# Two decode layers: w2's last block read over 96 partitions, and one load of V per layer split into 112 rows and four groups of 4 rows

## The chip, the core and the metric

One Trainium2 chip, one of its cores. The metric is the device time of one execution in microseconds (us): the median of the kernel's runs. The profile shown below is of one such execution.

## The reference

One token runs through attention, an MLP, attention and an MLP again, all in fp32, with the same weights in both layers:

```python
# x: 1x1x512; k_cache, v_cache: 1x32x4096x128; wq: 512x4096; wo: 4096x512
# w1: 512x1376; b1: 1376; w2: 1376x512; b2: 512
def _A_ref(x, k_cache, v_cache, wq, wo):
    q = (x @ wq).reshape(1, 1, 32, 128).transpose(0, 2, 1, 3)
    p = softmax(einsum("bhqd,bhkd->bhqk", q, k_cache) * 128 ** -0.5)
    return einsum("bhqk,bhkd->bhqd", p, v_cache).transpose(0, 2, 1, 3).reshape(1, 1, 4096) @ wo

def _B_ref(x, w1, b1, w2, b2):
    return gelu(x @ w1 + b1, approximate=True) @ w2 + b2

for _ in range(2):
    x = x + _A_ref(layernorm(x), k_cache, v_cache, wq, wo)
    x = x + _B_ref(layernorm(x), w1, b1, w2, b2)
```

K and V are 67 MB each and are read in both layers, apart from some parts that stay on the chip between the layers.

## The kernel before, in words

The 32 heads go in `G = 8` groups of four. For each group the kernel loads K (128 partitions of 64 KiB each), then V of the same size, and then one chunk of `wo` beside one of `wq`. TensorE makes the scores from K (`scores`, L232). VectorE and ScalarE make the softmax. V is then either summed by TensorE (`values`, L262) or, in most groups, weighted by ScalarE and VectorE (L269, L274) and added up by VectorE (L279). Layer 0 goes through the groups from 0 to 7, layer 1 back from 7 to 0, so that it starts with what is still on the chip.

All loads are issued by SyncE's queue, through `load` (L87), in the order in which the program was written (`tc.keep_in_program_order`). A load runs on the core's 16 DMA engines. Its end is counted on a semaphore, and the framework gives eight of these out in turn: a load has to wait until the load eight places ahead of it, which had the same semaphore, has landed. Most loads go into parts of one large tile, `arena`, and so wait for the last reader of that part too.

The last group of each layer (`final`) is what the change touches. Its V comes in smaller pieces: `LAST = ((0, 4), (4, 6), (6, 7))`, of 4 MiB, 2 MiB and 1 MiB (128 rows of 8 KiB), issued in `stream`, and the eighth chunk by `END_PARTS`. Behind it in the queue are `wo`'s last chunk, `w1` (in layer 0 only; it stays) and `w2`, cut up by `W2_PARTS`. The last piece of `w2` is block 10 of 11. It is the last load of the whole kernel in layer 1.

The MLP (`mlp`) takes its 1376 hidden units as four rows (`J = 4`) of 344, each padded to 352, so `w2` comes as 11 blocks of 128 units of which the last has 96 real units and 32 of zeros, spread over the quadrants. `hidden` (L355) makes four rows of hidden units in `HIDDEN` pieces of 4, 4 and 3 blocks; in the third piece each of the four rows has 88 columns. The second product (L414) goes block by block, four matmuls for each.

Of the kernel before, what the change touches and what calls it, by code (L numbers as in the profile page):

```python
# [17 lines left out]
P = 128  # L18
D = 512
H, S, DH = 32, 4096, 128  # L20
F = 1376
G = 8
J = 4
C = 8
FJ = F // J
FB = 11
EPS = 1e-5
U = 512
KEPT = 6

NC = 4 * U
# [3 lines left out]
SPARE = 2 * BLOCK + STAY  # L35
# [5 lines left out]
X_AT, B1_AT, B2_AT = 0, 8, 8 + FB  # L41
# [3 lines left out]
W2_AT = tuple(SPARE + U * (c % 8) for c in range(FB)), tuple(U * c for c in range(FB))  # L45
PITCH = 1024
W2_PARTS = ((0, 4), (4, 6), (6, 8), (8, 10), (10, FB)), ((0, 4), (4, 8), (8, 10), (10, FB))
HIDDEN = ((0, 4), (4, 8), (8, FB))
# [3 lines left out]
LAST = ((0, 4), (4, 6), (6, 7))  # L52
END_PARTS = ((0, 4),), ((0, 2), (2, 4))
LAST_IDLE = {3: 1, 5: 1, 6: 1}
WHOLE, HALVES = ((0, 8),), ((0, 4), (4, 8))
VAR_AT = 1
PAIRS = (0, 2, 4, 6), ((4, 6, 0, 2), (2, 0, 4, 6))


@with_exitstack  # L60
def decode_layers(ctx: ExitStack, tc: tile.TileContext, k, v, w, w1, w2, out):
    nc = tc.nc
# [20 lines left out]
    arena = const.tile([P, ARENA], F32, name="arena")  # L83

    def load(at, src):
        t = arena[:, at : at + src.shape[-1]]
        tc.keep_in_program_order(nc.sync.dma_start(t, src))  # L87
        return t

    def pin(ins):  # L90
        tc.keep_in_program_order(ins)

    def chunk(t, i=0):
        return t[:, NC * i : NC * (i + 1)].rearrange("p (j n) -> p j n", j=4)
# [28 lines left out]
    def part(src, g, a, b):  # L123

        return src[g][:, NC * a : NC * b]
# [23 lines left out]
    pM, pN = pO[:, 2 * P : 3 * P], pO[:, 3 * P :]  # L149
# [185 lines left out]
    def mlp(xs, s, w1_t, w2_t, xb, rows, fill, follow):  # L335
        hs, rstd = pH[layer], []
        if fill is None:
            nm, ss, _ = mean_of(xs, s, pN[:, 0:1], True)
            nm_s, nmr, cb, late = small("nm_s"), small("negm"), colsum, HIDDEN[0][1]
            nc.vector.tensor_copy(nm_s, nm)  # L340
        else:
            centred = small("xs", 8).rearrange("p (c i) -> p c i", i=2)
            nc.gpsimd.memset(centred[:, :, 1], 1.0)
            _, ss, _ = mean_of(xs, s, pN[:, 0:1], True, centred[:, :, 0])
        nc.gpsimd.tensor_tensor(xb, xs[:, :, 0], b2c, op=ALU.add)
        if fill is not None:
            xs = centred

        def hidden(i):
            at, first = hs[i], W1_AT[i]  # L350
            n = min(32 * HIDDEN[i][1], FJ) - 32 * HIDDEN[i][0]
            for c in range(4):
                for j in range(J):
                    f = first + n * (J * c + j)
                    pin(nc.tensor.matmul(at[32 * j : 32 * j + 2, :n], xs[:, c, :], w1_t[:, f : f + n],  # L355
                                         start=(c == 0), stop=(c == 3)))
                if i == 0 and c == VAR_AT:
                    rstd.append(rstd_of(ss, pN[:, 1:2], True))
                if i == 0 and c == VAR_AT and fill is None:
                    nc.gpsimd.tensor_tensor(nmr, nm_s, rstd[0], op=ALU.mult)  # L360
                    nc.gpsimd.tensor_scalar(cb[:, late:], colsum[:, late:], nmr, None, op0=ALU.mult)
                    nc.gpsimd.tensor_tensor(cb[:, late:], cb[:, late:], b1c[:, late:], op=ALU.add)

        def turned(i):
            ht = work.tile([P, 32 * 4], F32, name="pt")
            n = HIDDEN[i][1] - HIDDEN[i][0]
            pin(nc.vector.transpose(ht[:, : 32 * n], hs[i][:, : 32 * n]))  # L367
            return ht

        def gelu(i, ht):  # L370
            b0, b1_ = HIDDEN[i]
            n = b1_ - b0
            h, u, g = (small("gelu_" + k, FB)[:, b0:b1_] for k in "hug")
            if fill is not None:
                pin(nc.vector.scalar_tensor_tensor(u, of_32(ht, n), rstd[0], b1c[:, b0:b1_], op0=ALU.mult, op1=ALU.add))  # L375
                nc.gpsimd.tensor_copy(colsum[:, b0:b1_], of_32(ht, n, 1))
            elif i > 0:
                pin(nc.vector.scalar_tensor_tensor(u, of_32(ht, n), rstd[0], cb[:, b0:b1_], op0=ALU.mult, op1=ALU.add))
            else:
                pin(nc.vector.scalar_tensor_tensor(h, of_32(ht, n, 1), nm_s, of_32(ht, n), op0=ALU.mult, op1=ALU.add))  # L380
                pin(nc.vector.scalar_tensor_tensor(u, h, rstd[0], b1c[:, b0:b1_], op0=ALU.mult, op1=ALU.add))
            nc.scalar.activation(g, u, AF.Gelu_apprx_tanh)  # L382
            if fill is not None and b1_ == FB:
                nc.scalar.activation(small("m"), g[:, :1], AF.Exp, scale=0.0)
            return g

        if fill is not None:
            idle(fill, pS, 2 * P)
        hidden(0)
        if fill is None:  # L390
            hidden(1)
            pin(nc.vector.transpose(rows[:, P : 2 * P], rows[:, :P]))
        ht = turned(0)
        if fill is None:
            hidden(2)
        else:
            idle(fill, pO, 2 * P)
            idle(fill, pO, 2 * P)
        for i, (b0, b1_) in enumerate(HIDDEN):
            if i == 1 and fill is not None:  # L400
                for n in (512, 256):
                    idle(fill, pS, n)
                hidden(1)
                ht = turned(1)
                idle(fill, pS, 2 * P)
            g = gelu(i, ht)
            if fill is None and b1_ < FB:
                ht = turned(i + 1)
            for c in range(b0, b1_):
                if c == b0 + 2 and i == 1 and fill is not None:  # L410
                    hidden(2)
                    ht = turned(2)
                for j in range(J):
                    pin(nc.tensor.matmul(pM[32 * j : 32 * j + 1, :], g[:, c - b0 : c - b0 + 1],  # L414
                                         w2_t[c][:, P * j : P * (j + 1)], start=(c == 0), stop=(c == FB - 1)))
                for at, src in follow.get(c, ()):
                    load(at, src)
            if i == 1 and fill is not None:
                idle(fill, pS, 2 * P)
# [3 lines left out]
    nc.gpsimd.tensor_copy(b2c, ahead[:, B2_AT : B2_AT + 4])  # L423
    here = {}

    def stream(what, g, pieces, base):

        for a, b in pieces:
            t = load(base + NC * a, part(k if what == "k" else v, g, a, b))
            for c in range(a, b):  # L430
                here[what, g, c] = chunk(t, c - a)
                yield c, here[what, g, c]
# [7 lines left out]
    for layer in range(2):  # L440
# [23 lines left out]
        for n, g in enumerate(order):  # L464
            first, final = n == 0, n == G - 1
# [87 lines left out]
            if layer == 1 and n == 0:  # L553
                wo_t = chunk(arena[:, PAIR : PAIR + NC])
            elif final:
                at = PAIR + NC * layer
                for a, b in WO_PARTS[layer]:
                    load(at + U * a, of_w(wo_at(g), 1)[:, U * a : U * b])
                wo_t = chunk(arena[:, at : at + NC])
                if layer == 0:  # L560
                    load(HELD, w1[:, : W1_AT[1]])
                for a, b in W2_PARTS[layer][: 1 if layer == 0 else 4]:
                    load(W2_AT[layer][a], w2[:, U * a : U * b])
                if layer == 0:
                    load(HELD + W1_AT[1], w1[:, W1_AT[1] : W1_AT[2]])
            else:
                t = load(PAIR, of_w(wo_at(g) if layer == 0 else wq_at(g - 1), 2))
                wo_t, wq_next = (chunk(t, i) for i in ((0, 1) if layer == 0 else (1, 0)))
# [17 lines left out]
            if final:  # L586
                if layer == 0:
                    row_to_quadrants(row)
                    for a, b in W2_PARTS[0][1:3]:
                        load(W2_AT[0][a], w2[:, U * a : U * b])  # L590
                        if a == 4:
                            load(HELD + W1_AT[2], w1[:, W1_AT[2] :])
                idle(last_v, pO, 256)
# [25 lines left out]
        if layer == 0:  # L619
            first_k, next_wq = part(k, G - 2, 0, 1), of_w(wq_at(G - 2), 1)  # L620
            follow = {
                3: (*((W2_AT[0][a], w2[:, U * a : U * b]) for a, b in W2_PARTS[0][3:]),
                    (SPARE + NC - U, first_k[:, NC - U :])),
                5: ((SPARE + NC, next_wq[:, : 2 * U]),),
                7: ((SPARE + NC + 2 * U, next_wq[:, 2 * U :]),),
                9: ((SPARE, first_k[:, : 2 * U]),),
            }
# [16 lines left out]
def columns(a):  # L644

    return np.ascontiguousarray(a.reshape(J, 4, 32, -1).transpose(0, 2, 1, 3).reshape(P, 4, -1))
# [41 lines left out]
```

## Time and profile before

| | |
|---|---|
| runs | 673.79, 675.82, 676.31 us; median 675.82 us |
| the profiled execution | 673.33 us, of which the span from the first to the last instruction is 671.6 us |
| read from HBM in the span | 284.92 MB, 424 GB/s |
| DMA packets | 11556, of them 11528 on SyncE's queue |
| busy share of the span | TensorE 45%, VectorE 61%, ScalarE 32%, GpSimd 1% |
| granted TensorE clock, mean | 0.713 |

Times in the profile's rows are us from the start of the span. In the DMA part of the profile, a queue's row gives packets, MB, and the time that its packets took as a share of 16 engines over the window that was asked for. The row marked DMA gives the busy share of the 16 engines in 40 equal slices of the window, in tenths (9 is 90% or more). A packet is one row of a load, or the small mark behind the last row on an engine that counts up the semaphore; those marks are the packets under 512 B.

### The profile page before, as it was taken

Reading aid. Unit: us, or ns where it says so; the run is one execution under the profiler, and the core shown is the slowest. Engines: PE = TensorE matmul, PEld = TensorE weight load, DVE = VectorE, ACT = ScalarE, POOL = GpSimd, SP = SyncE. Lnnn points to the kernel's source line nnn. Section 1 sums busy time; section 2 is a strip of 40 time slices with the busy share of each in tenths; the row PEclk is TensorE's granted clock in tenths of the full one; section 3 lists DMA queues with packets and bytes.
Section 4 is the critical chain, followed back from the end, with each engine's and each line's share of the span. In section 5 each row is a group of like instructions: output and inputs, shape, how many; then the busy total and the mean of one; then the engine's idle time right before and its main releaser. Section 6 shows DMA issues by size and latency. Waiting matters only on the chain.

```text
span 671.6 us, 6013 instructions
## 1 busy us (share of the span) xinstructions
PE 299.7 (45%) x2236; PEld 79.7 (12%) x2236; DVE 407.1 (61%) x510; ACT 215.4 (32%) x697; POOL 5.2 (1%) x26
## 2 busy tenths in 40 slices
PE   1511703415116053165768986704316025065597
PEld 1000100101001010011114311101001001011124
DVE  3059679498696886971322313288597694973513
ACT  0047074190560823802011200083290650910010
POOL 1000000000000000000000000000000000000000
PEclk9965755757558557578689998655757559557799
DMA  9999999999999999999999999999999999999997
GB/s 377 437 437 438 435 437 437 403 461 437 437 437 397 444 426 434 433 429 426 425 415 399 422 422 438 437 433 433 431 433 437 437 430 402 462 426 414 431 414 286
DMA packets 11556, 285.29 MB, mean 425 GB/s; under 512 B 1284, under 2 KB 1288, under 8 KB 3720
## 3 DMA queue, kind: packets, MB, share of 16 engines
q1 hardware_dynamic: 11528, 284.92, 99.1%
q8 instruction: 17, 0.28, 0.2%
q14 instruction: 11, 0.09, 0.0%
HBM read 284.92 MB, written 0.00 MB: 424 GB/s over the span
## 4 chain that ended last, share of the span: by engine, by line
DMA 64%; PE 17%; DVE 15%; issue 1%; another core or an unknown queue 1%; SPq 1%; ACT 0%; DVEq 0%; ACTq 0%
DMA arena<-in_v 37%; DMA arena<-in_k 24%; PE pS L232 8%; DVE arena L274 7%; PE pO L262 5%; DMA arena<-in_w 4%; DVE arena L279 3%; DVE arena L311 2%; PE pO L283 1%; DVE arena L287 1%; DVE arena L215 1%; SPq L87 1%; PE pB L323 1%; DVE arena L309 0%
## 5 line engine op out<-in xcount | busy, mean ns | idle before, releaser
L269 ACT ACTIVATE arena<-arena,pt 128x128 f32<-128x128 f32 x640 | 188.0, 387 | 50.8 <-DMA arena<-in_v 48.1
L232 PE MATMUL pS<-arena,smalls 128*8 128x512 f32 x1024 | 147.0, 727 | 78.4 <-DMA arena<-in_k 74.3
L279 DVE TENSOR_TENSOR arena<-arena 128x4096 f32<-128x4096 f32 x30 | 132.6, 4420 | 0.3
L274 DVE TENSOR_TENSOR arena<-arena,pt 128x2048 f32<-128x2048 f32 x40 | 89.0, 2287 | 36.8 <-DMA arena<-in_v 35.7
L217 PE MATMUL pS<-arena,smalls 128*128 128x512 f32 x20 | 20.7, 1140 | 202.5 <-DVE arena L215 202.5
L244 ACT ACTIVATE arena<-pS,smalls 128x512 f32<-128x512 f32 x16 | 12.4, 777 | 289.4 <-DVE smalls L243 289.4
L287 DVE STREAM_TRANSPOSE arena<-pO 128x512 f32<-128x512 f32 x16 | 11.5, 717 | 97.4 <-PE pO L262 61.9
L262 PE MATMUL pO<-arena,pt 128*4 128x512 f32 x368 | 48.9, 666 | 11.8 <-DMA arena<-in_v 11.0
L232 PEld LDWEIGHTS pS<-arena,smalls 128*8 128x8 f32 x1024 | 29.8, 102 | 198.6 <-issue 177.3
L236 DVE TENSOR_REDUCE smalls<-pS 128x1 f32<-128x512 f32 x16 | 11.0, 687 | 64.1 <-PE pS L232 64.1
L215 DVE SCALAR_TENSOR_TENSOR arena<-arena,smalls 128x512 f32<-128x512 f32 x45 | 33.8, 752 | 1.6
L311 DVE SCALAR_TENSOR_TENSOR arena<-arena,smalls 128x512 f32<-128x512 f32 x39 | 29.3, 752 | 1.4
L217 PEld LDWEIGHTS pS<-arena,smalls 128*128 128x128 f32 x20 | 5.0, 311 | 206.2 <-DVE arena L215 206.2
L315 PE MATMUL pB<-arena,smalls 128*1 128x512 f32 x26 | 14.7, 648 | 29.0 <-DVE arena L311 29.0
L246 PE MATMUL pO<-ident,arena 128*128 128x128 f32 x64 | 13.4, 344 | 28.1 <-ACT arena L244 27.8
L574 DVE TENSOR_TENSOR arena<-arena 128x2048 f32<-128x2048 f32 x10 | 22.9, 2292 | 0.3
L382 ACT ACTIVATE smalls<-smalls 128x4 f32<-128x4 f32 (+1 forms) x6 | 1.2, 205 | 44.0 <-DVE smalls L375 25.6
L262 PEld LDWEIGHTS pO<-arena,pt 128*4 128x4 f32 x368 | 9.8, 93 | 44.8 <-issue 42.4
L250 DVE STREAM_TRANSPOSE smalls<-smalls 128x32 f32<-128x32 f32 x16 | 3.4, 212 | 17.5 <-ACT arena L244 17.5
L246 PEld LDWEIGHTS pO<-ident,arena 128*128 128x128 f32 x64 | 8.4, 167 | 42.1 <-ACT arena L244 36.7
L244 ACT ACT_TABLE_LOAD x1 | 1.3, 1283 | 36.9 <-DVE smalls L243 36.9
L438 PE MATMUL pS<-arena,ident 128*8 128x256 f32 (+1 forms) x34 | 11.9, 454 | 0.5 <-DVE pt L367 0.5
(115 smaller groups left out, 183.6 us busy)
## 6 DMA issues: line engine op xcount, KB each, us to landing
arena<-in_w SPq DMA_DIRECT2D x13, 2048.0 KB, 12.5
arena<-in_k SPq DMA_DIRECT2D x6, 4096.0 KB, 21.3
arena<-in_v SPq DMA_DIRECT2D x2, 4096.0 KB, 25.1
arena<-in_w SPq DMA_DIRECT2D x6, 1024.0 KB, 30.9
arena<-in_v SPq DMA_DIRECT2D x2, 2048.0 KB, 37.0
arena<-in_k SPq DMA_DIRECT2D x2, 2048.0 KB, 13.4
arena<-in_w SPq DMA_DIRECT2D x7, 512.0 KB, 9.3
arena<-in_v SPq DMA_DIRECT2D x3, 1024.0 KB, 46.3
```

Of the source, the lines that this page charges most:

```text
L215: pin(nc.vector.scalar_tensor_tensor(t, wt[:, c, :], xc[:, c : c + 1], t, op0=ALU.mult, op1=ALU.add))
L217: pin(nc.tensor.matmul(at, one.to_broadcast([P, P]), t, start=True, stop=True))
L232: pin(nc.tensor.matmul(pS[32 * j : 32 * j + C, :], z[:, j, C - 1 - c : 2 * C - 1 - c], kt[:, j, :], start=(c == 0), stop=(c == C - 1)))
L246: nc.tensor.transpose(pT[:, b].rearrange("p j r -> p (j r)"), p[:, P * b : P * (b + 1)], ident)
L262: nc.tensor.matmul(pO[32 * j : 32 * j + 4, :], pt[:, j, c, :], by_head(vt)[:, j], start=(i == 0), stop=(i == of - 1))
L269: nc.scalar.activation(own, own, AF.Copy, scale=pt[:, j, c, b : b + 1])
L274: nc.vector.tensor_tensor(own, own, weight, op=ALU.mult)
L279: pin(nc.vector.tensor_tensor(a, a, b, op=ALU.add))
L287: nc.vector.transpose(ot[:, :512], pO)
L311: pin(nc.vector.scalar_tensor_tensor(t, wt[:, d, :], on[:, d : d + 1], t, op0=ALU.mult, op1=ALU.add))
L315: pin(nc.tensor.matmul(pB[0:1, :], one, t, start=n == 0, stop=n == G - 2))
L574: pin(nc.vector.tensor_tensor(total, total, other, op=ALU.add))
```

## The change

It has two parts.

1. The 1376 hidden units are taken in their own order, without padding inside: blocks 0 to 9 have 128 real units, and block 10 has the 96 that are left. `w2`'s block 10 is then loaded over 96 partitions in place of 128 (`load_w2`), and its matmuls contract over 96. In `hidden`'s third piece the four rows have 96, 96, 96 and 64 columns in place of four times 88. The layouts of `w1`, `w2` and `b1` in HBM are made to fit.
2. The piece (6, 7) of `LAST`, 128 rows of 8 KiB, is loaded by five transfers (`DEALT`): one of 112 rows and four of 4 rows. This is so in both layers.

```diff
+FULL = F - P * (FB - 1)
+DEALT = (0, 112), (112, 116), (116, 120), (120, 124), (124, 128)
...
+    def load_w2(layer, a, b):
+        at, rows = W2_AT[layer][a], FULL if b == FB else P
+        pin(nc.sync.dma_start(arena[:rows, at : at + U * (b - a)], w2[:rows, U * a : U * b]))
...
         def hidden(i):
             at, first = hs[i], W1_AT[i]
-            n = min(32 * HIDDEN[i][1], FJ) - 32 * HIDDEN[i][0]
+            b0, b1_ = HIDDEN[i]
+            ns = [32 * (b1_ - b0 - (b1_ == FB and j == J - 1)) for j in range(J)]
             for c in range(4):
-                for j in range(J):
-                    f = first + n * (J * c + j)
+                for j, n in enumerate(ns):
+                    f = first + sum(ns) * c + sum(ns[:j])
...
+                used = FULL if c == FB - 1 else P
...
                 for j in range(J):
-                    pin(nc.tensor.matmul(pM[32 * j : 32 * j + 1, :], g[:, c - b0 : c - b0 + 1],
-                                         w2_t[c][:, P * j : P * (j + 1)], start=(c == 0), stop=(c == FB - 1)))
+                    pin(nc.tensor.matmul(pM[32 * j : 32 * j + 1, :], g[:used, c - b0 : c - b0 + 1],
+                                         w2_t[c][:used, P * j : P * (j + 1)], start=(c == 0), stop=(c == FB - 1)))
+                if layer == 0 and c == 3:
+                    for a, b in W2_PARTS[0][3:]:
+                        load_w2(0, a, b)
...
+    def load_dealt(at, src):
+
+        t = arena[:, at : at + src.shape[-1]]
+        for a, b in DEALT:
+            pin(nc.sync.dma_start(t[a:b], src[a:b]))
+        return t
...
         for a, b in pieces:
-            t = load(base + NC * a, part(k if what == "k" else v, g, a, b))
+            dealt = what == "v" and (a, b) == LAST[-1]
+            t = (load_dealt if dealt else load)(base + NC * a, part(k if what == "k" else v, g, a, b))
```

The rest of the diff replaces `load` by `load_w2` where `w2`'s other pieces are loaded, and the layouts in `kernel`.

On SyncE's queue, at the end of layer 1, this stood before. Sizes are rows x fp32 elements, and the names in brackets are what a load waits for: `DMAHW` and a number is one of the eight semaphores, that is, the load eight places ahead.

```order
L87 DMA arena<-in_v 128x4096 [waits Activation_49]
L87 DMA arena<-in_v 128x2048 [waits Activation_49]
L87 DMA arena<-in_v 128x1024 [waits Activation_49] x2
L87 DMA arena<-in_w 128x1024 [waits DMAHW1_49,PE_49]
L87 DMA arena<-in_w 128x512 [waits DMAHW2_49]
L87 DMA arena<-in_w 128x512 [waits DMAHW3_49]
L87 DMA arena<-in_w 128x2048 [waits DMAHW4_49]
L87 DMA arena<-in_w 128x2048 [waits DMAHW5_49]
L87 DMA arena<-in_w 128x1024 [waits DMAHW6_49]
L87 DMA arena<-in_w 128x512 [waits DMAHW7_49]
```

The same place of the queue in the changed kernel:

```order
L89 DMA arena<-in_v 128x4096 [waits Activation_49]
L441 DMA arena<-in_v 112x2048 [waits Activation_49]
L441 DMA arena<-in_v 4x2048 x2
L441 DMA arena<-in_v 4x2048 [waits DMAHW5_49]
L441 DMA arena<-in_v 4x2048 [waits DMAHW6_49]
L89 DMA arena<-in_v 128x1024 [waits DMAHW7_49,Activation_49]
L89 DMA arena<-in_v 128x1024 [waits DMAHW0_49,Activation_49]
L89 DMA arena<-in_w 128x1024 [waits DMAHW1_49,PE_49]
L89 DMA arena<-in_w 128x512 [waits DMAHW2_49]
L89 DMA arena<-in_w 128x512 [waits DMAHW3_49]
L96 DMA arena<-in_w 128x2048 [waits DMAHW4_49]
L96 DMA arena<-in_w 128x2048 [waits DMAHW5_49]
```

Four small loads now take four places among the eight, so the loads behind them wait for a load that stands less far ahead in bytes: the first 128x512 load of `wo` waited for the first half of K before, and waits for the 112 rows of V now.

More of the change, by code (lines that the diff above doesn't have):

```diff
@@ L562, in decode_layers @@
                 for a, b in W2_PARTS[layer][: 1 if layer == 0 else 4]:
-                    load(W2_AT[layer][a], w2[:, U * a : U * b])
+                    load_w2(layer, a, b)
                 if layer == 0:
@@ L589, in decode_layers @@
                     for a, b in W2_PARTS[0][1:3]:
-                        load(W2_AT[0][a], w2[:, U * a : U * b])
+                        load_w2(0, a, b)
                         if a == 4:
@@ L621, in decode_layers @@
             follow = {
-                3: (*((W2_AT[0][a], w2[:, U * a : U * b]) for a, b in W2_PARTS[0][3:]),
-                    (SPARE + NC - U, first_k[:, NC - U :])),
+                3: ((SPARE + NC - U, first_k[:, NC - U :]),),
                 5: ((SPARE + NC, next_wq[:, : 2 * U]),),
@@ L651 @@
         x=A_x, k=A_k_cache, v=A_v_cache, wq=A_wq, wo=A_wo, w1=B_w1, b1=B_b1, w2=B_w2, b2=B_b2).items()}
-    pad = 32 * FB - FJ
-    w2 = np.pad(a["w2"].reshape(J, FJ, D), ((0, 0), (0, pad), (0, 0)))
-    b1 = np.pad(a["b1"].reshape(J, FJ), ((0, 0), (0, pad)))
-    w1 = columns(a["w1"]).reshape(P, 4, J, FJ)
+    w2 = np.pad(a["w2"], ((0, P * FB - F), (0, 0))).reshape(FB, P, D)
+    b1 = np.pad(a["b1"], (0, P * FB - F)).reshape(FB, P)
+    w1 = columns(a["w1"])
     wq = columns(a["wq"]).reshape(P, 4, G, J, J, 32)
@@ L663 @@
         (X_AT, columns(a["x"])[:, :, 0]),
-        (B1_AT, b1.reshape(J, FB, 32).transpose(0, 2, 1).reshape(P, FB)),
+        (B1_AT, b1.T),
         (B2_AT, columns(a["b2"])[:, :, 0]),
@@ L671 @@
         w=w,
-        w1=np.concatenate([w1[..., 32 * a : 32 * b].reshape(P, -1) for a, b in HIDDEN], axis=1),
-        w2=w2.reshape(J, FB, 32, D).transpose(0, 2, 1, 3).reshape(P, FB * D),
+        w1=np.concatenate([w1[:, c, f : f + 32] for a, b in HIDDEN for c in range(4) for j in range(J)
+                           for f in range(P * a + 32 * j, min(P * b, F), P)], axis=1),
+        w2=w2.transpose(1, 0, 2).reshape(P, FB * D),
     )
```

## The prediction

> **What bounds the kernel now.** I read the page first, for the share of the DMA engines, then the chain of waits at the end of each layer.
>
> ```profile
> span 671.6 us, 6013 instructions
> DMA  9999999999999999999999999999999999999997
> q1 hardware_dynamic: 11528, 284.92, 99.1%
> q8 instruction: 17, 0.28, 0.2%
> q14 instruction: 11, 0.09, 0.0%
> ```
>
> The loads' queue holds 99.1% of all 16 engines over the span: no compute engine bounds this kernel, the transfer of 285 MB does. What is left to ask is whether the engines stay busy where the layers meet, since there the chain runs through many small steps. A table by stage around that place, columns as printed (the last two are DMA share and GB/s):
>
> ```profile
> 355.00:369.00 14.00, 11.78 (x230) 6.06 (x218) 2.98 (x14) 2.10 (x5) 1.42 (x6) 1.00 1.01 397
> 369.00:383.00 14.00, 12.71 (x124) 4.72 (x124) 6.99 (x28) 1.65 (x4) 0.55 (x1) 1.00 1.04 419
> 383.00:397.00 14.00, 12.58 (x98) 2.83 (x102) 1.17 (x4) 2.45 (x5) 0.00 (x0) 1.00 1.00 423
> ```
>
> The share stays at 1.00 or above (a packet is booked where it starts). So work saved on an engine in layer 0 isn't lost in a hole at the boundary; it reaches the end. The chain of waits at the end of layer 0, then of layer 1:
>
> ```profile
> 360.18 7.25 DMA arena<-in_w
> 367.57 1.00 PE pO L414 x24
> 368.65 0.33 DVE pt L632
> ...
> 656.04 11.41 DMA arena<-in_w
> 667.46 0.14 issue
> 667.59 1.00 PE pO L414 x24
> 668.62 0.29 DVE arena L640
> ```
>
> Both layers end on a load of `w2`, and its landing sets the end of the kernel.
>
> A load has landed when its slowest engine is done. How far apart the engines are is seen where they run out of work, from 665.2 to 668.4 (slices of 80 ns):
>
> ```profile
> DMA  4999496858487675646252322911110000000000
> q1 hardware_dynamic: 204, 0.51, 40.6%
> ```
>
> They don't stop together. The row falls from about 666.2 and reaches 0 at slice 30, that is 665.2 + 30 x 0.08 = 667.6. The queue's packets take 40.6% of 3.2 us x 16 = 20.8 engine-us; shared evenly this would be over at 665.2 + 20.8 / 16 = 666.5. So the last engine runs 1.1 us behind the mean, and no re-dealing in this layer can bring more than that. One cause of the spread is seen in the instruction fetches: whole blocks, each on one engine. One of them in a window of 1 us (667.2 to 668.2):
>
> ```profile
> q8 instruction: 1, 0.02, 6.9%
> q1 hardware_dynamic: 16, 0.02, 6.7%
> ```
>
> One fetch holds one engine for 0.069 x 16 = 1.10 us, and there are 17 of them. Before V's last pieces in layer 0, from 0 to 349, there had been six:
>
> ```profile
> q8 instruction: 6, 0.10, 0.1%
> q14 instruction: 5, 0.04, 0.0%
> ```
>
> So some engines must be about 1.1 us late there too, and at least five of 16 have had no fetch at all.
>
> **The change part by part.** `w2`'s block 10 loses 32 rows of 2 KiB, two on each engine (96 rows are six on each of 16). The last rows of just this size are in the 1 us window above: 6.7% x 16 = 1.07 us for 16 packets, of which 12 are rows (0.02 MB); 0.09 us a row. That is 0.18 us off every engine in each layer, 0.35 us in all, all of it on the path, as the DMA is full. Block 10's matmuls still number four and the hidden columns are 12 x 96 + 4 x 64 = 16 x 88: nothing, and they stand ahead of the waits of 7.25 and 11.41 us, or in the last 1.00 us unchanged.
>
> The split moves no byte, but deals the rows anew. First, the price of a row of 8 KiB, in a window of 1 us in which only these rows run (346.2 to 347.2):
>
> ```profile
> DMA packets 59, 0.40 MB, mean 401 GB/s; under 512 B 10, under 2 KB 10, under 8 KB 10
> q1 hardware_dynamic: 59, 0.40, 99.9%
> ```
>
> 15.98 engine-us for 49 rows and their marks: 0.326 us a row. Next, on how many engines four rows go. The store of the result is the one transfer of 4 rows in the trace (669.9 to 670.5):
>
> ```profile
> DMA packets 8, 0.00 MB, mean 3 GB/s; under 512 B 4, under 2 KB 8, under 8 KB 8
> ```
>
> Four rows and four marks: four engines were used, one row each. The 80 loads make the other 1280 of the page's marks, 16 each. So I take four engines for each of the four transfers, and 16 for the 112 rows. On which four, no row tells. If they are always the same, these get 7 + 4 = 11 rows in place of 8, the other twelve get 7: +3 x 0.326 = +0.98 us on four engines, -0.33 us on twelve, in each layer. If the four transfers went to other engines each time, all would have 8 again and nothing would change.
>
> [...]
>
> The bounds follow. If the four are at least 1.30 us (0.98 + 0.33) ahead of the last, the last engine is 0.33 us earlier in each layer: -0.65 us. If one of the four is the last itself: +1.95 us. With `w2`: from -1.00 to +1.60 us. Which end? Six fetches of 1.10 us before the piece in layer 0 leave most engines at a lead of about that size, and the tail row says that at 666.3, 1.3 us before the last, about a third of the engines have stopped. Four engines picked at random would seldom all be among them. [...] I take the early end, narrowly.
>
> SyncE issues eight transfers more, at 2.23 / 5 = 0.45 us each:
>
> ```profile
> 623.48 2.23 SPq L87 DMA_DIRECT2D arena<-in_v  x5
> 628.81 28.84 SPq L87 DMA_DIRECT2D arena<-in_w  x7
> SPq L87 <- DMA arena<-in_v: 17.0, 4, 9.4
> ```
>
> The queue issues in layer 1's tail within 28.84 us, most of it waits for loads eight places ahead, so 4 x 0.45 = 1.8 us is covered as long as loads are queued. What covers it is thinner now. Before, the first 128x512 of `wo` waited for a half of K with over 8 MB behind that; now it waits for the 112 rows, with two loads of V and one of `wo` behind, 1.5 MB, 3.6 us at 437 GB/s. The waits for the small loads come after it, within some 1.3 us. Against that stands the delay from issue to landing. The first load, 1056 KB, shows it:
>
> ```profile
> 0.72 4.95 DMA arena<-in_w
> arena<-in_w SPq DMA_DIRECT2D x1, 1056.0 KB
> GB/s 377 437 437 438 435 437 437 403 461 437 437 437 397 444 426 434 433 429 426 425 415 399 422 422 438 437 433 433 431 433 437 437 430 402 462 426 414 431 414 286
> ```
>
> 1.08 MB take 2.5 us at 437 GB/s, so 2.5 us are delay. 3.6 us are enough for the last engine. An engine that is over 1 us ahead may run dry for up to about 1 us, which it has to spare: I take nothing, and 0 to 1 us for the range. In layer 0, three loads of 1 MiB are behind the 112 rows, twice as much. TensorE has five loads to wait for at V's seventh chunk in place of one; its waits cost 51 ns each where they stand alone, ahead of the same 7.25 and 11.41 us:
>
> ```profile
> L414 PEldq EVENT_SEMAPHORE  x6: 51/51/51, 359.4 to 667.5; - x6
> ```
>
> Sum: -0.35 - 0.65 = -1.00 us. The profiled execution took 673.33 us (span 671.6 and 1.7 around it), so 672.3 us for one like it. It stands 2.5 us below the median of the three runs, 675.82; at the median the sum gives 674.8 us.
>
> **The rivals.** (a) One of the four engines is late: +1.60 us at worst, 677.4 us, slower than before. It decides from where the latest of the four leads the last engine by less than 0.98 us. [...] (b) The four transfers don't go to the same engines, or the freed time is lost to other engines that are just as late: only `w2` counts, 675.5 us. (c) The queue runs dry at the thinner place in layer 1: up to +1 us on all engines if the issue comes later than 3.6 us after the 112 rows; 675.8 to 676.8 us. (d) All four transfers go to one engine: 7 + 16 = 23 rows, 15 x 0.326 = +4.9 us less its lead of up to 2.4 us, in each layer: 680 to 685 us. The store's four marks speak against it. (e) Each small transfer is served alone, with its own delay of 2.5 us: 8 x 2.5 = +20 us, 695 us. Against it: from 656 to 664 loads of 0.25 to 1 MiB follow each other without a hole.
>
> ```profile
> 656.00:664.00 8.00, 6.99 (x122) 3.49 (x124) 2.98 (x14) 0.00 (x0) 0.28 (x2) 1.00 1.03 412
> ```
>
> [...]
>
> **How the numbers follow.** The forecast case has a chance of 0.45, (a) 0.33, (b) 0.10, (c) 0.06, (d) 0.04, (e) 0.02. A difference of 0.5%, 3.4 us, is about what a measurement of this kernel can tell from no change. Even full levelling, 2 x 1.1 + 0.35 = 2.6 us, doesn't reach it. So faster by that much gets 0.03, for scatter alone, slower 0.07, for (d), (e) and scatter, no difference 0.90. The range ends at (a)'s worst, 677.4 us. Below it takes the forecast less the distance of the median to the lowest run (2.0 us) and a little more: 672.6 us.
>
> **What would show it.** In the changed kernel the marks fall into 16 for the 112 rows and four for each small transfer: 1284 + 8 x 4 = 1316 packets under 512 B. If the forecast holds, the fall of the tail row takes less than the 1.4 us of before (666.2 to 667.6), and `w2`'s wait ends earlier in both layers. If (a) holds, a few engines run on alone in the tail for up to 1 us. If (c) holds, the DMA row of the last 20 us shows a hole. The prediction would be wrong if the issue of the extra transfers moved loads of the next layer, so that the share between 369 and 397 fell below 1.

## The result and the profile after

The changed kernel takes 686.05 us (median of 6 runs, 685.07 to 688.43), the one before 673.85 us beside it (6 runs). The ratio is 1.0179, 95% interval 1.0164 to 1.0194: 12 us slower, and well above the range that was forecast.

The page of the changed kernel, its span, the DMA row and the GB/s row in 40 slices, and the packets:

```profile
span 683.2 us, 6028 instructions
DMA  9999999999999999999999999999999999999996
GB/s 378 464 445 431 423 430 434 425 432 430 430 430 413 448 431 430 437 414 436 424 318 352 414 417 456 406 458 435 430 430 434 430 431 430 430 431 424 431 306 251
DMA packets 11524, 285.16 MB, mean 417 GB/s; under 512 B 1316, under 2 KB 1320, under 8 KB 3688
```

The DMA engines are as busy as before, and yet they move less: 318 and 352 GB/s in the 21st and 22nd slice, 306 in the 39th, where the row of before has 415, 399 and 414. These are the two places of the split load. Here they are by stage, first the kernel before, then the changed one (the last two columns are DMA share and GB/s). In layer 1 the same work stands about 11 us later in the changed kernel.

```profile
345.00:354.00 9.00, 8.54 (x91) 2.44 (x84) 1.67 (x5) 0.00 (x0) 0.00 (x0) 1.00 1.00 414
646.00:656.00 10.00, 9.37 (x64) 2.54 (x64) 1.01 (x6) 1.49 (x2) 0.00 (x0) 1.00 0.98 408
```

```profile
345.00:354.00 9.00, 6.64 (x40) 1.19 (x32) 0.00 (x0) 0.00 (x0) 0.00 (x0) 0.88 1.00 237
657.00:667.00 10.00, 5.14 (x40) 1.27 (x32) 0.00 (x0) 0.00 (x0) 0.00 (x0) 1.00 1.01 230
```

A share of 1.00 at 237 GB/s in place of 414: hardly any engine waits for work, but each row takes nearly twice as long. The packets of the changed kernel say the same; a window of 1 us in which only 8 KiB rows run (350 to 351) has 28 of them beside 4 marks, where 346.2 to 347.2 had 49 before:

```profile
DMA packets 32, 0.23 MB, mean 229 GB/s; under 512 B 4, under 2 KB 4, under 8 KB 4
q1 hardware_dynamic: 32, 0.23, 109.5%
```

It isn't only the rows of the split load. By their size, the packets in the trace can be told apart: rows of 16 KiB belong to the piece (4, 6) ahead of it, a load of 128 rows in both kernels. From 344.5 to 347 there are 15 of them in either kernel; they took 0.62 us each before and 1.04 us in the changed kernel. In layer 1 rows of 4 KiB, all of them from loads of 128 rows, took 0.16 us before (653 to 659) and 0.32 us in the changed kernel (660 to 666).

In the two windows of 9 and 10 us, 9 x (414 - 237) / 414 = 3.8 us and 10 x (408 - 230) / 408 = 4.4 us are lost. The chain of waits of the changed kernel shows where the rest comes to light:

```profile
367.10 6.07 DMA arena<-in_w
373.31 1.02 PE pO L422 x24
...
635.39 32.06 DMA arena<-in_v
667.45 0.14 issue
667.58 1.53 PE pO L268 x8
...
677.81 2.45 PE pO L422 x85
...
680.29 0.29 DVE arena L658
```

Layer 0's last matmuls start at 373.31 in place of 367.57, 5.7 us late. V's last load in layer 1 lands at 667.45 in place of 656.04, 11.4 us late. In layer 1 the chain no longer passes through `w2`: its last rows come in until about 679, while TensorE is still at the blocks before (677.81 to 680.26). The kernel's last step ends 13.1 us after V's landing, in place of 12.9 us before, so V's delay reaches the end nearly whole. What layer 0 loses beyond its slow window shows at the layers' boundary, first before, then changed:

```profile
364.00:374.00 10.00, 8.11 (x163) 3.85 (x166) 4.23 (x18) 1.69 (x3) 0.84 (x3) 1.00 1.00 372
374.00:384.00 10.00, 9.27 (x70) 3.07 (x66) 3.63 (x14) 2.04 (x4) 0.00 (x0) 1.00 1.07 444
```

```profile
364.00:374.00 10.00, 8.98 (x196) 5.02 (x198) 1.80 (x9) 1.76 (x4) 1.22 (x5) 1.00 0.92 319
374.00:384.00 10.00, 9.28 (x117) 3.16 (x110) 4.54 (x17) 0.92 (x3) 0.55 (x1) 1.00 0.99 360
```

8.2 MB in 20 us became 6.8 MB, about 3 us of transfer, of which some 0.8 us is won back by 411. With the two slow windows this makes 3.8 + 2.3 + 4.4 = 10.5 of the 11.6 us by which the span grew. Here the share does fall, to 0.92. That loads are issued late because compute is late can't be all of it: `low64` and `deal112_16` below lose no less in layer 0's slow window (210 and 206 GB/s from 345 to 354), and their share from 363 to 373 is 1.00 and 1.01, where the changed kernel has 0.93. The split of the change alone (`deal_only`) has 0.89. So five transfers in place of two or three may have a part in these 2.3 us; no run settles it.

### The profile page after: what moved, and what is told of

It reads as the page before. It is cut to its first block, busy times and chain, and to the rows that moved or that the text cites. A ratio compares the mean times of both kernels' runs of the same rounds, so it can differ in the third digit from the quotient of the medians.

```text
span 683.2 us, 6028 instructions
## 1 busy us (share of the span) xinstructions
PE 303.7 (44%) x2236; PEld 81.5 (12%) x2236; DVE 407.1 (60%) x510; ACT 215.3 (32%) x697; POOL 5.2 (1%) x26
## 2 busy tenths in 40 slices
DMA packets 11524, 285.16 MB, mean 417 GB/s; under 512 B 1316, under 2 KB 1320, under 8 KB 3688
## 4 chain that ended last, share of the span: by engine, by line
DMA 64%; PE 22%; DVE 11%; issue 1%; another core or an unknown queue 1%; SPq 1%; ACT 0%; DVEq 0%; ACTq 0%
DMA arena<-in_k 48%; DMA arena<-in_v 14%; PE pS L238 13%; DVE arena L317 4%; PE pO L268 3%; DMA arena<-in_w 2%; PE pO L289 1%; DVE arena L280 1%; DVE arena L293 1%; DVE arena L221 1%; DVE arena L315 1%; DVE arena L285 1%; PE pO L422 1%; SPq L89 1%
## 5 line engine op out<-in xcount | busy, mean ns | idle before, releaser
L238 PE MATMUL pS<-arena,smalls 128*8 128x512 f32 x1024 | 145.4, 721 | 78.2 <-DMA arena<-in_k 74.0
L268 PE MATMUL pO<-arena,pt 128*4 128x512 f32 x368 | 50.6, 702 | 19.6 <-DMA arena<-in_v 18.3
L457 PE MATMUL pS<-arena,ident 128*8 128x256 f32 (+1 forms) x34 | 13.6, 512 | 0.5 <-DVE pt L374 0.5
## 6 DMA issues: line engine op xcount, KB each, us to landing
arena<-in_k SPq DMA_DIRECT2D x2, 2048.0 KB, 11.6
```

Source lines behind the costliest of these rows:

```text
L238: pin(nc.tensor.matmul(pS[32 * j : 32 * j + C, :], z[:, j, C - 1 - c : 2 * C - 1 - c], kt[:, j, :], start=(c == 0), stop=(c == C - 1)))
L268: nc.tensor.matmul(pO[32 * j : 32 * j + 4, :], pt[:, j, c, :], by_head(vt)[:, j], start=(i == 0), stop=(i == of - 1))
```

## Experiments

Three theories stood at the start. P: a load that has not 128 rows slows itself and the loads in flight beside it; that the engines get into each other's way while they write was the author's guess at how. Q: five transfers thin the queue. W: `w2`'s 96 rows are to blame. All differences below are between medians, against the kernel before, run beside them (673.51 to 674.05 us). The ratios and their 95% intervals are worked out from the single runs and need not be the ratio of two medians.

### The change taken apart

`w2` alone: the changed kernel with the split undone.

```diff
-            t = (load_dealt if dealt else load)(base + NC * a, part(k if what == "k" else v, g, a, b))
+            t = load(base + NC * a, part(k if what == "k" else v, g, a, b))
```

> The changed kernel with V's piece (6, 7) as one load of 128 rows again: only w2's block 10 over 96 rows is left of the change. Theory P (the rows of a load that has not 128 rows don't come to the engines as those of 128 do, and the engines then stand in each other's way while they write, so that every row in flight takes about twice as long): nearly all of the loss is gone; the 96 rows are short, six rows of 0.09 us an engine, so -0.35 us if they are not slowed and about +1 us if they take twice as long: ratio 0.999 to 1.002. Theory Q (five transfers in place of one, with eight semaphores, leave the queue thin): -0.35 us, ratio 0.999. Theory W (w2's 96 rows are what costs): the loss of 12 us stays, ratio 1.018.

675.22 us, +1.2 us, ratio 1.0016 (1.0006 to 1.0025). W falls. But the sum's -0.35 us for the bytes saved isn't there either. The tail of the loads agrees with P's case that they are slowed: from 666 to 670.3 rows of 2 KiB took 0.108 us in place of 0.086 before (664 to 667.8), and rows of 4 KiB, which belong to loads of 128 rows, 0.18 in place of 0.16. The hidden columns and the layouts changed too in this kernel and were not run apart.

The split alone: the kernel before with `DEALT`. Of the edits from here on only the lines that differ between the kernels are shown; the rest of `load_dealt` and its call in `stream` stand as in the change.

```diff
+DEALT = (0, 112), (112, 116), (116, 120), (120, 124), (124, 128)
...
+        for a, b in DEALT:
+            pin(nc.sync.dma_start(t[a:b], src[a:b]))
```

> The kernel before with nothing but the split of V's piece (6, 7) into 112 rows and four transfers of 4 rows. P: the loss is here, +10 to +12 us, ratio 1.015 to 1.018, and the DMA part of the profile shows a share of about 1.00 at some 235 GB/s for 8 to 10 us at the end of each layer. Q: also +10 to +12 us, but with a DMA share well under 1 there. W: within 0.2% of before.

685.22 us, +11.2 us, ratio 1.0169 (1.0151 to 1.0187). With `w2`'s 1.2 us this is the whole loss. Its windows, as in the changed kernel, have a full share, where Q had one well under 1:

```profile
345.00:354.00 9.00, 5.88 (x44) 1.05 (x36) 0.00 (x0) 0.00 (x0) 0.00 (x0) 1.00 0.98 226
657.00:667.00 10.00, 5.92 (x48) 1.49 (x40) 0.00 (x0) 0.00 (x0) 0.00 (x0) 1.00 1.01 232
```

Five transfers of 128 rows, cut by columns:

```diff
+PARTS = (0, 1024), (1024, 1280), (1280, 1536), (1536, 1792), (1792, 2048)
...
+        for a, b in PARTS:
+            pin(nc.sync.dma_start(t[:, a:b], src[:, a:b]))
```

> The kernel before with V's piece (6, 7) as five transfers too, but all of 128 rows, cut by columns: 4 KiB and four times 1 KiB a row. The queue of SyncE, the eight semaphores and what waits for them stand as with the split by rows. P: nothing is slowed beyond the shorter rows' own price (32 rows an engine of 1 KiB in place of 8 KiB in one: under 0.5 us a layer), ratio 0.999 to 1.003. Q: the same loss as with the split by rows, ratio 1.010 to 1.018. [...]

674.78 us, +0.7 us, ratio 1.0012 (1.0001 to 1.0024). Eight transfers more in SyncE's queue, the same places among the eight semaphores, and nearly nothing is lost. With the full share above, Q falls as the cause of the loss. The windows hold 402 and 400 GB/s:

```profile
345.00:354.00 9.00, 9.00 (x77) 2.12 (x69) 0.98 (x3) 0.00 (x0) 0.00 (x0) 0.86 1.02 402
657.00:667.00 10.00, 8.75 (x176) 5.07 (x178) 3.90 (x18) 0.12 (x1) 1.29 (x5) 1.00 1.01 400
```

Two halves of 64 rows:

```diff
+DEALT = (0, 64), (64, 128)
```

> The kernel before with V's piece (6, 7) as two transfers of 64 rows, partitions 0 to 63 and 64 to 127, 4 rows on each of 16 engines. [...] P in a plainer form (only rows that aren't a multiple of 4 on an engine collide): no change, 0.999 to 1.002. [...]

682.82 us, +8.8 us, ratio 1.0133 (1.0116 to 1.0150). No transfer is small here (512 KiB each), there is one transfer more a layer in place of four, and 64 rows are four for each of 16 engines if all are used. That it costs nearly as much as the split rules out P's plainer form, Q and a price of small transfers as the main cause. What is left is that it matters which partitions the rows go to, or a cost of any load that hasn't 128 rows, whichever its partitions are (theory N).

### Which partitions

The next pair has the same three sizes in the same order, 64, 32 and 32 rows. The place of the 64 rows differs, and with it that of the first 32, which go to partitions 64 to 95 or to 0 to 31. If the place matters, the two kernels differ; by N they take the same time.

`low64`:

```diff
+DEALT = (0, 64), (64, 96), (96, 128)
```

`mid64`:

```diff
+DEALT = (32, 96), (0, 32), (96, 128)
```

> The kernel before with V's piece (6, 7) as three transfers: rows 0 to 63, 64 to 95, 96 to 127. The control for the next kernel. Two halves of 64 rows had cost 8.8 us, so 2.2 us for each 64 rows, and if cost goes by rows 1.1 us for each 32. [...]

> The same three sizes as the control, but the 64 rows are partitions 32 to 95, and the two transfers of 32 rows are 0 to 31 and 96 to 127. [...]

`low64` 683.15 us, +9.1 us, ratio 1.0134 (1.0114 to 1.0153). `mid64` 679.87 us, +5.8 us, ratio 1.0086 (1.0066 to 1.0105). The intervals don't touch: moving 64 rows by 32 partitions takes off 3.3 us, and N falls. The first of the 64 rows start at about 344.1 in both. The 2 us around that, first `low64`, then `mid64`:

```profile
343.50:345.50 2.00, 2.00 (x20) 0.50 (x16) 0.00 (x0) 0.00 (x0) 0.00 (x0) 0.72 1.14 311
```

```profile
343.50:345.50 2.00, 2.00 (x16) 0.42 (x12) 0.00 (x0) 0.00 (x0) 0.00 (x0) 0.50 0.96 401
```

The packets show it row by row. From 344 to 345 a row of 8 KiB took 0.31 us in `mid64`, as in the kernel before, and 0.54 us in `low64`; the rows of 16 KiB beside them, of the load of 128 rows ahead, took 0.62 and 0.98 us. So the 64 rows at 32 to 95 slow nothing in that 1 us; the 5.8 us come with the two loads of 32 rows behind them.

To part the side that is written from the side that is read, the pair was run again with the rows of HBM exchanged. The keys of this piece of V then stand in a permuted order, so these two kernels leave out the right pairing of weights and keys there and serve for the time alone.

`cross_low`:

```diff
+DEALT = (0, 64, 32), (64, 96, 0), (96, 128, 96)
...
+        for a, b, r in DEALT:
+            pin(nc.sync.dma_start(t[a:b], src[r : r + b - a]))
```

`cross_mid`, with the same loop:

```diff
+DEALT = (32, 96, 0), (0, 32, 64), (96, 128, 96)
```

> As the control low64 (64, 32 and 32 rows, to partitions 0 to 63, 64 to 95, 96 to 127), but the 64 rows are read from rows 32 to 95 of V in HBM and the first 32 from rows 0 to 31: the keys of this piece stand in a permuted order, which leaves the transfers' sizes and all compute as they were. It parts the side that is read from the side that is written. [...] Theory H (the rows of HBM that are read): as mid64, +5 to +6.5 us, ratio 1.007 to 1.010.

> As mid64 (64 rows to partitions 32 to 95, 32 to 0 to 31, 32 to 96 to 127), but the 64 rows are read from rows 0 to 63 of V in HBM and the next 32 from rows 64 to 95; keys permuted as in the kernel beside it. P: as mid64, +5 to +6.5 us, ratio 1.007 to 1.010. H: as low64, +8 to +10 us, ratio 1.012 to 1.015.

`cross_low` 683.42 us, +9.9 us, ratio 1.0156 (1.0128 to 1.0183). `cross_mid` 679.69 us, +6.2 us, ratio 1.0091 (1.0065 to 1.0116). The cost goes with the partitions that are written, not with the rows that are read.

### Which of the transfers, and how much of them

112 rows and one transfer of 16; and 112 rows and four transfers of 4 rows that lie four partitions apart. If the 112 rows carry the loss, it stays in both. If the transfers of 4 rows carry it, most of it goes in the first; if it comes from their rows lying next to each other, in the second.

`deal112_16`:

```diff
+DEALT = (0, 112), (112, 128)
```

`deal_step`:

```diff
+        pin(nc.sync.dma_start(t[:112], src[:112]))
+        for i in range(4):
+            pin(nc.sync.dma_start(t[112 + i : 128 : 4], src[112 + i : 128 : 4]))
```

> The kernel before with V's piece (6, 7) as 112 rows and one transfer of 16 rows, one on each engine. [...]

> [...] The queue is the same as with the split of the change (+11.2 us). [...]

`deal112_16` 683.97 us, +9.9 us, ratio 1.0137 (1.0116 to 1.0159). `deal_step` 685.03 us, +11.0 us, ratio 1.0161 (1.0137 to 1.0185), as the split of the change. So the small transfers are not the main cost, nor is it that the four rows of a transfer lie next to each other. The 112 rows are in all three kernels, with most of the loss; they were not run without some companion, so that they alone carry it is argued from these.

Then an eighth of the bytes (only the last 1 KiB of each row is split), and three times the bytes (the piece (4, 6) is split too):

`tail256`, with the `DEALT` of the change:

```diff
+        pin(nc.sync.dma_start(t[:, :1792], src[:, :1792]))
+        for a, b in DEALT:
+            pin(nc.sync.dma_start(t[a:b, 1792:], src[a:b, 1792:]))
```

`deal_more`, the kernel with the split alone and:

```diff
+            dealt = what == "v" and (a, b) in LAST[1:]
```

> The kernel before with V's piece (6, 7) as 128 rows of 7 KiB, and only the last 1 KiB of each row by 112 rows and four times 4 rows: six transfers, an eighth of the bytes split. P: the loss goes with the time for which split rows are in flight, so about an eighth of 11.2 us, plus some 0.8 us as the five column pieces had: +1.5 to +3.5 us, ratio 1.002 to 1.005. Theory F (a fixed price for each load that hasn't 128 rows): all of the loss stays, +9 to +13 us, ratio 1.013 to 1.019.

> The kernel before with both V's piece (4, 6) (rows of 16 KiB, 2 MiB) and (6, 7) split into 112 rows and four times 4 rows, so three times the bytes. P: the loss grows with the bytes, about three times 11.2 us less what overlaps of the neighbours' slowing: +25 to +34 us, ratio 1.037 to 1.050. F: twice as many such loads, +20 to +23 us, ratio 1.030 to 1.034.

`tail256` 677.16 us, +3.7 us, ratio 1.0051 (1.0035 to 1.0067). `deal_more` 697.45 us, +23.9 us, ratio 1.0349 (1.0331 to 1.0368). An eighth, one and three parts of the bytes cost 3.7, 11.2 and 23.9 us. The loss grows with the bytes that are split, but not in proportion, and both runs lie just outside what P gave as numbers: 0.2 us above 3.5, 1 us below 25. A fixed price for each such load (+9 to +13 us for `tail256`) is excluded by `tail256` alone; the 23.9 us of `deal_more` lie between F's +20 to +23 and P's +25 to +34 and don't part them. What the part is that doesn't go with the bytes was not settled. A line through 3.7 and 11.2 us puts it at about 1 us a layer, after the 0.35 us that five transfers cost in `cols5`; this is an estimate from two runs.

## Why the prediction was wrong

**The step that failed** is the price of the split: "0.326 us a row", taken from 8 KiB rows of loads of 128 rows, and used for loads of 112 and 4. In the changed kernel, by the same working, 28 such rows took 1.095 x 16 = 17.5 engine-us, 0.63 us a row in that window. So the split, forecast at -0.65 us, cost 11.2 us alone. And not only the split rows were slow: the neighbours in flight too (0.62 to 1.04 us for 16 KiB, 0.16 to 0.32 us for 4 KiB), in stretches of 9 us in layer 0 and 10 us in layer 1, though the split load itself is 2.4 us of transfer at 437 GB/s. The sum had the rows moved between engines, +0.98 us here and -0.33 us there, as if an engine's speed were its own. That a row's price depends on which partitions are being written beside it (rows of 16 KiB took 0.62 us beside the 64 rows at 32 to 95, 0.98 us beside those at 0 to 63) was in no term and no rival.

**What stands in its place.** The cost goes with the partitions that a load is written to. Two halves cost 8.8 us. The 64 rows at 32 to 95 took 0.31 us a row, as in the kernel before, against 0.54 at 0 to 63, and the rows of HBM made no difference (683.42 us with them exchanged beside 683.15, 679.69 beside 679.87). Loads of 128 rows beside a misplaced one are slowed as well (0.98 us in place of 0.62 for rows of 16 KiB). Why some partitions cost and others don't is not shown: no run shows which engine wrote which row. And for the 112 rows it is argued that their place is what costs, as no run had them at other partitions.

**`w2`'s block 10**: forecast -0.35 us, measured +1.2 us alone. The bytes were saved (285.16 MB against 285.29). That the same slowing ate them is what the tail of `w2_only` suggests (0.108 us for its rows of 2 KiB, where the sum took 0.09, and 0.18 for its neighbours of 4 KiB). In the whole change `w2` doesn't decide the end of layer 1 at all, by the chain above.

**The spread of the engines.** 1.1 us between the last engine and the mean was read rightly from the tail, and is too small to matter beside 12 us. Worked out in the same way, the last engine is 1.9 us behind in the changed kernel (676.2 to 679.2) and 1.7 us in `w2_only` (667.2 to 670.1), which has no split; so the tail that was named as a sign doesn't tell the forecast from rival (a). Whether four engines with three rows more would have levelled anything can't be said: no split without the slowing was run. So whether the four engines were early or late, on which the forecast and rival (a) turned, stays open. No run shows which four took the small transfers, nor that they were ahead of the others, so the sum's -0.65 us was the author's estimate; what the runs showed in its place is the +11.2 us of `deal_only`.

**What was right.** The marks: 1284 + 32 = 1316 under 512 B, so each transfer of 4 rows ran on four engines; rival (d) is out, and that its 680 to 685 us come nearest to the measured time is chance. SyncE's time and the places among the eight semaphores cost little (`cols5`, +0.7 us), near the nothing that the sum took; rival (c), an empty queue in layer 1, is out, as the share is full where the rate falls (1.01 from 657 to 667). Rival (e), a delay for each small transfer, is out too: 16 rows as one transfer in place of four changed 11.2 into 9.9 us, 1.3 us for six transfers in all, and the two intervals overlap. Eight more transfers of 128 rows on SyncE's queue cost 0.7 us together, 0.1 us each (`cols5`). What is lost in layer 0 does reach the end, as the prediction had it: of the 11.4 us by which V's last load is late in layer 1, 5.7 us were there at the end of layer 0.

**The warning that was named**: the share between 369 and 397 did fall below 1, to 0.95 in the first of the two windows, where it was 1.04 before:

```profile
369.00:383.00 14.00, 12.44 (x214) 5.18 (x209) 5.61 (x21) 1.90 (x4) 1.02 (x4) 1.00 0.95 325
```

But that is a small part: about 2.3 us are lost around there. The main loss lies in the two windows with a full share, where the warning doesn't look.

## What to carry to other kernels

In a kernel that the DMA bounds, as this one, keep every load at 128 partitions, even if that moves padding (`w2`'s 96 rows in place of 128 gave +1.2 us); cut loads by columns (five pieces, +0.7 us), not by rows (two pieces, +8.8 us, and five, +11.2 us). Read GB/s beside the share of the DMA engines: here a share of 1.00 stood beside 237 GB/s in place of 414, and the loads of 128 rows in flight were slowed as well. A duration from one shape of transfer doesn't price another shape: the 0.326 us a row from loads of 128 rows became 0.63 with the split.

## What the runs showed of the hardware

- That a load's rows are a whole multiple of 16 isn't enough: 1 MiB a layer in two halves of 64 rows cost +8.8 us over two layers, 112 rows with 16 +9.9 us, and the kernel with `w2`'s 96 rows of 2 KiB +1.2 us.
- With 112 rows and four times 4, the rate fell to 226 to 237 GB/s at a share of 0.98 to 1.01, from 408 to 414, for 9 to 10 us, about four times as long as the split load's own transfer (2.4 us at 437 GB/s).
- Loads of 128 rows beside such a load are slowed too: rows of 16 KiB from 0.62 to 1.04 us, rows of 4 KiB from 0.16 to 0.32 us.
- The same 64 rows, with the same companions in size, cost 3.3 us less at partitions 32 to 95 than at 0 to 63 (3.7 us in the pair with exchanged sources).
